# Linear attention and a gated feed-forward layer on one core: block 0's decay in its mask, WO by column halves, projection 0 in half tiles

## The chip, the cores and the metric

The kernel runs on one core of a Trainium2 chip. Its engines each run their own instruction stream in order: TensorE (PE; its weight loads are listed as PEld), VectorE (DVE), ScalarE (ACT), GpSimd (POOL) and SyncE (SP). SP, ACT and POOL can issue DMA transfers; they share 16 DMA engines. Engines wait for each other through semaphores. The metric is the time of one execution on the device in microseconds (us); lower is better.

## The reference

```python
for b in range(nb):                      # attention, block after block
    qb, kb, vb = (q[:, :, sl], k[:, :, sl], v[:, :, sl])
    intra = einsum('bhic,bhjc->bhij', qb, kb) * Dmask      # lam ** (i - j), i >= j
    intra = einsum('bhij,bhjd->bhid', intra, vb)
    inter = einsum('bhid,bhde->bhie', qb * lam_pow, kv_state)
    out[:, :, sl] = intra + inter
    kv_state = lam_block * kv_state + einsum('bhsd,bhse->bhde', kb * rev_pow, vb)
x = out.transpose(0, 2, 1, 3).reshape(B * S, H * D)        # 3072 x 512
gate = 1.0 / (1.0 + np.exp(-(x @ w_gate)))
val = x @ w_val
result = gate * val @ w_out                                # 3072 x 512
```

Batch 4, 8 heads, sequence 768, head size 64; `w_gate` and `w_val` are 512 x 1536, `w_out` is 1536 x 512. `lam` holds one decay per head, from 0.97 to 0.99. All tensors are float32 in memory; the kernel computes its matmuls in bf16.

## The kernel before

The sequence is cut into six blocks of C = 128 positions (`NSTEP`). A block takes all four batches at once, so that its feed-forward work has 512 tokens. For each block n the stages are:

- Load q, k, v as bf16 (`load`, L83, on POOL's queue). Block 0's k of batches 0 and 1 come as float32 on SP (`load_hw`, L134) and are cast on VectorE (`cast_hw`, L226).
- Transpose q and k: by TensorE for blocks 0 and 1 (`t_`, L202, evacuated by `e_q` and `e_k`), by DMA from block 2 on (`xbar`, L229, issued on SP). `e_q` (L209) scales q by lam^(i+1) (`lamq`).
- Scores (`piece_s`, L238) into two PSUM banks per batch; product with the mask on VectorE (`piece_m`, L249). Because q carries lam^(i+1), the mask needs only lam^(-j-1) below the diagonal (`make_mask`, L190, from `pk` and `tri`).
- Attention output: the part from the state (`piece_i`, L255, not for block 0) and the part from v (`piece_a`, L266); evacuation to XT (`piece_x`, L278); the new state (`piece_c`, L285, with k scaled by `kds` in `piece_kd`, L116, on ScalarE).
- Gate and value (`piece_gv`, L308): twelve units, each four gate matmuls and four value matmuls of 512 columns, a sigmoid on ScalarE and a product on VectorE. The PSUM pool `ps_ff` has three banks, which gate, value and output tiles take in turn; attention has a pool of five (`ps_at`).
- Projection (`piece_po`, L324): for each batch tile 12 matmuls against WO, a copy on ScalarE, an output DMA on SP.

The order on each engine is the program order, written out by hand. First comes the prologue (L340 to L379): block 0's attention for batches 0 and 1, then 2 and 3, with filler matmuls (`zeros`) between. Then the remaining loads are put on POOL's queue (L383 to L395). Then comes `plan` (L412 to L502), a list of units with small pieces behind each: block 0's gate and value units, with block 1's transposes, scores and masks behind units 7 to 11 and its attention (`att(1)`) behind unit 11; four of block 1's units; projection 0; block 1's other units; then block by block. In blocks 2 to 5 the attention of the next block stands behind unit 11 and before the projection.

POOL's queue in order: q, k, q, v of block 0; WG and WV in five parts; block 1's k and q with WG/WV parts between; v of block 1; WO in two halves by rows of 128 (`load_wo`, L107); k and q of block 2. A DMA on this queue was issued, from the ninth on, only after the one eight before it had landed: for instance, the issue at 42.45 us waited for block 1's v. From block 2 on, `next_loads` (L403) puts two DMA transposes on SP, then two small copies on POOL (`gate`, L399) that wait for them, and behind these the loads of the next v, k and q. SP also issues the outputs, so transposes and outputs stand in one queue.

`tables_late` (L182) computes `kds` and `dec`, loads the sigmoid table and swaps the two 64-partition halves of `lamq` and `dec` by four DMAs on SP into `lamqs` and `decs`, which batches 2 and 3 use from block 1 on (`swapped`).

Of the kernel before, what the change touches and what calls it, by code (L numbers as in the profile page):

```python
# [16 lines left out]
def kernel(  # L17
# [26 lines left out]
    hwp = ctx.enter_context(tc.tile_pool(name="hwp", bufs=4))  # L44
# [26 lines left out]
    def swapped(n, b):  # L71
        return n > 0 and b >= NB2
# [7 lines left out]
    def rows_of(u):  # L80
        return slice(u * 64, (u + 1) * 64)
# [22 lines left out]
        nc.gpsimd.dma_start(out=WG[:, :, fs], in_=wg_r[:, :, fs])  # L104
        nc.gpsimd.dma_start(out=WV[:, :, fs], in_=wv_r[:, :, fs])

    def load_wo(f0, f1):  # L107
        fs = slice(f0, f1)
        nc.gpsimd.dma_start(out=WO[:, fs, :], in_=wo_r[:, fs, :])

    KD = {}

# [13 lines left out]
    jn = const.tile([128, 2], FP32, tag="jn")  # L126
    ip1 = const.tile([128, C], FP32, tag="ip1")
    tri = const.tile([128, C], FP32, tag="tri")
    Sb = stp.tile([128, HP, B, 64], BF16, tag="Sb", name="Sb")
    lam_bc = const.tile([128, H], FP32, tag="lam_bc")  # L130

# [2 lines left out]
    def load_hw(c, b, eng):  # L134
# [9 lines left out]
    nc.scalar.preload_act_table_set("natural_log_exp_and_others")  # L144
    nc.vector.memset(ident, 0.0)
    nc.vector.memset(Sb, 0.0)  # L146
    nc.vector.memset(tri, 0.0)
# [14 lines left out]
    load_gv(2, 4)  # L162
    load_gv(4, 6)

    lnp = const.tile([128, HP], FP32, tag="lnp")
# [3 lines left out]
    lamq = const.tile([128, HP, C], BF16, tag="lamq")  # L169
    for hp in range(HP):  # L170
        nc.scalar.activation(lamq[:, hp, :], ip1, AF.Exp, scale=lnp[:, hp:hp + 1])
    lamqs = const.tile([128, HP, C], BF16, tag="lamqs")
    lnl = const.tile([128, H], FP32, tag="lnl")
    nc.scalar.activation(lnl, lam_bc, AF.Ln)
    pk = const.tile([128, H], FP32, tag="pk")
    nc.scalar.activation(pk, lnl, AF.Exp, scale=jn[:, 0:1])
    kds = const.tile([128, H], FP32, tag="kds")
    dec = const.tile([128, HP], FP32, tag="dec")
    decs = const.tile([128, HP], FP32, tag="decs")
# [10 lines left out]
    def make_mask():  # L190
        nc.vector.tensor_tensor(
            out=mask, in0=tri.unsqueeze(1).unsqueeze(1).to_broadcast([128, 2, HP, C]),
            in1=pk.rearrange("p (hp u) -> p u hp", u=2).unsqueeze(3).to_broadcast([128, 2, HP, C]),
            op=ALU.mult)

# [6 lines left out]
    def t_(c, n, bs):  # L202
        ps = ps_at.tile([128, len(bs), HP, C], BF16, name="t" + c, tag="ps")
        for i, b in enumerate(bs):
            for hp in range(HP):
                nc.tensor.transpose(ps[:, i, hp, :], T_[c, n][:, b, 2 * hp:2 * hp + 2, :], ident)  # L206
        (tqs if c == "q" else tks)[n, bs[0]] = ps

    def e_q(n, bs):  # L209
        w = len(bs)  # L210
        src = tqs[n, bs[0]] if n < FIRST_XBAR else QT[n][:, bs[0]:bs[0] + w]
        t = trsb.tile([128, 2, HP, C], BF16, tag="QS", name="QS")
        nc.vector.tensor_tensor(out=t[:, :w], in0=src,  # L213
                                in1=(lamqs if swapped(n, bs[0]) else lamq).unsqueeze(1).to_broadcast([128, w, HP, C]), op=ALU.mult)
        for i in range(w):
            QS[n, bs[i]] = t[:, i]

# [8 lines left out]
    def cast_hw(c, b):  # L226
        nc.vector.tensor_copy(T_[c, 0][:, b], H32[c, b])
# [21 lines left out]
    def piece_m(n, b):  # L249
        MT[n, b] = mtp.tile([128, 2, HP, C], BF16, tag="MT", name="MT")  # L250
        for u in range(2):
            nc.vector.tensor_tensor(out=MT[n, b][:, u], in0=SP[n, b][u],  # L252
                                    in1=mask[:, 1 - u if swapped(n, b) else u], op=ALU.mult)

    def piece_i(n):  # L255
        for b in range(B):
# [67 lines left out]
    def piece_po(n, tt, cuts=(0, 512)):  # L324
        ob = osb.tile([128, DM], FP32, tag="ob", name="ob")
        rows = out[tt * S + n * C:tt * S + (n + 1) * C, :]
        for j, (c0, c1) in enumerate(zip(cuts, cuts[1:])):
            po = ps_ff.tile([128, DM], FP32, name="po", tag="ff")
            for ft in range(NFT):
                nc.tensor.matmul(po[:, :c1 - c0], lhsT=HT[n, ft][:, tt * 128:(tt + 1) * 128],  # L330
                                 rhs=WO[:, ft, c0:c1], start=(ft == 0), stop=(ft == NFT - 1))
            if j:
                nc.vector.tensor_copy(ob[:, c0:c1], po[:, :c1 - c0])
            else:
                nc.scalar.copy(ob[:, c0:c1], po[:, :c1 - c0])  # L335
            nc.sync.dma_start(out=rows[:, c0:c1], in_=ob[:, c0:c1])

# [6 lines left out]
            nc.tensor.matmul(zps, lhsT=Sb[:, 0, 0:2, :], rhs=Sb[:, 0:2], start=True, stop=True)  # L344

    zeros(9)
    for b in range(2):
        cast_hw("k", b)
        t_("k", 0, [b])
        e_k(0, [b])  # L350
        zeros(3 if b == 0 else 0)
    make_mask()
    for b in range(2):
        t_("q", 0, [b])
        e_q(0, [b])
    zeros(1)
    for b in range(2):
        piece_s(0, [b])
        piece_m(0, b)
    t_("k", 0, [2, 3])  # L360
    e_k(0, [2, 3], parts=2)
    zeros(2)
    t_("q", 0, [2, 3])
    e_q(0, [2, 3])
    tables_late()
    zeros(3)
    for b in range(2, 4):
        piece_s(0, [b])
        piece_m(0, b)
    for b in range(2):  # L370
        piece_a(0, [b])
        piece_x(0, [b], nc.scalar)
# [44 lines left out]
    def gv(n, ft, *more):  # L417
        unit(lambda: piece_gv(n, ft), *more)

    def po(n, tt, *more, cuts=(0, 512)):  # L420
        unit(lambda: piece_po(n, tt, cuts), *more)

    def pair(f, n, bp):
        return lambda: f(n, [2 * bp, 2 * bp + 1])
# [38 lines left out]
    for n in range(1, NSTEP):  # L463
        nx = n + 1
        more = {i: [] for i in range(NFT)}
# [10 lines left out]
        if nx < NSTEP - 1:  # L476
            more[5].append(lambda nx=nx: make_kd(nx))
        if n == 1:
            for ft in range(4):
                gv(1, ft, *[lambda: next_loads(2)] if ft == 3 else [])  # L480
            for tt in range(B):
                po(0, tt, *[lambda: next_loads(3)] if tt == 3 else [])
            gv(1, 4, *more[3])
            gv(1, 5)
            gv(1, 6, *more[4])
            gv(1, 7, *more[5])
            gv(1, 8, *more[6])
            gv(1, 9, *more[7])
            gv(1, 10, *more[8])
            gv(1, 11, *more[9], *more[10], *more[11])  # L490
        else:
            for ft in range(NFT):
                gv(n, ft, *more[ft])
        for tt in range(B):
            last = n == NSTEP - 1 and tt == B - 1
            more = [lambda n=n: next_loads(n + 3)] if tt == B - 1 and n + 3 < NSTEP else []
            po(n, tt, *more, cuts=(0, 256, 512) if last else (0, 512))

    for f, more in plan:
        f()  # L500
# [32 lines left out]
```

## Time and profile before

| What | Value |
|---|---|
| Median of 3 runs | 230.18 us (230.18 to 230.3) |
| Profiled execution, time | 230.23 us |
| Profiled execution, span from first to last instruction | 228.4 us |
| Mean granted TensorE clock | 1.000 |
| First gate matmul (L313) of block 0 | 17.82 us |
| First gate matmul of block 1 | 45.81 us |
| Projection 0 (L330) | 52.73 us, 10.5 us long |
| Last copy of the output (L333) | 225.36 us, 0.42 us long |
| DMA packets under 512 B | 94,080 of 104,083 |
| Bytes on POOL's queue (q0) and on SP's (q1) | 13.90 MB and 11.15 MB |

The page divides the span into engines' busy time, and then gives groups of instructions by line: how many, their busy time, the mean of one, and the idle time before them with what ended it. The costliest groups on the engines beside TensorE:

```profile
L322 DVE TENSOR_TENSOR ht<-sg,vp 128x512 bf16<-128x512 bf16 x72 | 49.4, 687 | 105.0 <-PE vp L319 101.4
L316 ACT ACTIVATE sg<-gp 128x512 bf16<-128x512 f32 x72 | 42.9, 596 | 66.0 <-PE gp L313 63.3
L335 ACT COPY ob<-po 128x512 f32<-128x512 f32 (+1 forms) x24 | 13.8, 576 | 47.3 <-PE po L330 47.3
L252 DVE TENSOR_TENSOR MT<-sp,mask 128x512 bf16<-128x512 f32 x48 | 30.4, 682 | 0.6 <-PE sp L244 0.5
```

The number before the bar is the count; then come busy us and the mean in ns; then the idle us and their releaser. Such idle time costs nothing where the engine isn't the one that sets the end.

### The profile page before, as it was taken

How to read it: one execution, taken by the hardware profiler on the slowest of the kernel's cores; microseconds unless marked ns; L12 is line 12 of the kernel's file. 1: busy time of each engine (PE TensorE's matmuls, PEld its weight loads, DVE VectorE, ACT ScalarE, POOL GpSimd, SP SyncE). 2: the span in 40 equal slices, each digit the busy share in tenths (PEclk: the TensorE clock that was granted, in tenths of full speed). 3: DMA queues.
4: the chain of work that ended last, by engine and by line, in shares of the span. 5: the costliest groups of instructions: out<-in, count | busy, mean ns of one | idle time of the engine just before them, and what ended most of it. 6: DMA issues, size and time to landing. Idle time of an engine off the chain costs nothing.

```text
span 228.4 us, 4108 instructions
## 1 busy us (share of the span) xinstructions
PE 218.3 (96%) x1642; PEld 107.2 (47%) x1668; DVE 100.9 (44%) x177; ACT 98.2 (43%) x207; POOL 57.9 (25%) x73
## 2 busy tenths in 40 slices
PE   7779999999999999999999999999999999999994
PEld 2444455544444644444554444454444454444443
DVE  2863367862038730368530368630268600343300
ACT  5465635932245832338542438642433342433221
POOL 7958669200192039004900030000000000000000
PEclk9999999999999999999999999999999999999999
DMA  7999999999999969994993739003100012100022
GB/s 113 156 166 196 174 173 176 201 181 160 221 158 152 192 99 146 211 167 78 137 160 122 168 65 91 3 27 114 46 0 3 0 37 103 46 0 0 3 92 93
DMA packets 104083, 25.31 MB, mean 111 GB/s; under 512 B 94080, under 2 KB 101120, under 8 KB 104064
## 3 DMA queue, kind: packets, MB, share of 16 engines
q0 software_dynamic: 81280, 13.90, 82.0%
q1 hardware_dynamic: 22640, 11.15, 20.7%
q8 instruction: 13, 0.21, 0.4%
q14 instruction: 6, 0.05, 0.1%
q10 hardware_dynamic: 144, 0.00, 0.0%
HBM read 28.32 MB, written 6.29 MB: 151 GB/s over the span
## 4 chain that ended last, share of the span: by engine, by line
PE 89%; DVE 3%; DMA 3%; issue 2%; POOL 1%; POOLq 0%; DVEq 0%
PE po L330 27%; PE vp L319 27%; PE gp L313 27%; DMA qb<-in_q_dram 3%; PE sp L244 3%; PE op L273 2%; DVE MT L252 2%; PE op L262 1%; PE cp L291 1%; DVE XT L283 1%; PE tq L206 1%; POOL kb L92 0%; PE tk L206 0%; DVE QS L213 0%; POOL qb L92 0%
## 5 line engine op out<-in xcount | busy, mean ns | idle before, releaser
L322 DVE TENSOR_TENSOR ht<-sg,vp 128x512 bf16<-128x512 bf16 x72 | 49.4, 687 | 105.0 <-PE vp L319 101.4
L319 PE MATMUL vp<-XT,WV 128*128 128x512 bf16 x284 | 73.5, 379 | 0.4
L313 PE MATMUL gp<-XT,WG 128*128 128x512 bf16 x274 | 72.1, 379 | 1.4 <-DVE XT L283 0.5
L316 ACT ACTIVATE sg<-gp 128x512 bf16<-128x512 f32 x72 | 42.9, 596 | 66.0 <-PE gp L313 63.3
L330 PE MATMUL po<-WO,ht 128*128 128x512 bf16 (+1 forms) x294 | 62.7, 370 | 0.4 <-issue 0.2
L330 PEld LDWEIGHTS <-ht 128*128 128x128 bf16 x300 | 29.0, 98 | 32.3
L319 PEld LDWEIGHTS <-WV 128*128 128x128 bf16 x288 | 28.2, 98 | 34.0
L313 PEld LDWEIGHTS <-WG 128*128 128x128 bf16 x288 | 27.0, 98 | 32.6 <-issue 0.8
L335 ACT COPY ob<-po 128x512 f32<-128x512 f32 (+1 forms) x24 | 13.8, 576 | 47.3 <-PE po L330 47.3
L252 DVE TENSOR_TENSOR MT<-sp,mask 128x512 bf16<-128x512 f32 x48 | 30.4, 682 | 0.6 <-PE sp L244 0.5
L121 ACT ACTIVATE kd<-kb,kds 128x128 bf16<-128x128 bf16 (+1 forms) x72 | 23.7, 402 | 0.0
L401 POOL COPY gates<-kt 128x1 bf16<-128x1 bf16 x4 | 0.7, 187 | 55.8 <-DMA kt<-kb 55.8
L283 ACT CAST XT<-op 128x512 bf16<-128x512 f32 x21 | 11.0, 596 | 5.5 <-PE op L273 5.5
L92 POOL DMA_DIRECT2D vb<-in_v_dram x7 | 10.7, 1530 | 2.6 <-issue 1.2
L98 POOL DMA_DIRECT2D qb<-in_q_dram x10 | 9.0, 916 | 3.1 <-DMA vb<-in_v_dram 2.1
L344 PE MATMUL zps<-Sb 128*128 128x512 bf16 x22 | 8.1, 499 | 1.6 <-DVE Sb L146 1.5
L98 POOL DMA_DIRECT2D kb<-in_k_dram x10 | 8.9, 902 | 1.0 <-DMA WG<-in_moe_w_gate_dram 0.6
L92 POOL DMA_DIRECT2D qb<-in_q_dram x7 | 8.4, 1202 | 0.8 <-POOLq L517 0.8
L273 PE MATMUL op<-MT,vb 128*64 128x128 bf16 x192 | 7.1, 221 | 0.4 <-DVE MT L252 0.3
L92 POOL DMA_DIRECT2D kb<-in_k_dram x6 | 7.0, 1166 | 0.0
L300 DVE SCALAR_TENSOR_TENSOR Sb<-Sb,dec,cp 128x128 bf16<-128x128 bf16 x16 | 5.5, 342 | 3.2 <-PE cp L291 3.2
L273 PEld LDWEIGHTS <-vb 128*64 128x64 bf16 x192 | 5.7, 110 | 1.6 <-DMA vb<-in_v_dram 0.7
(47 smaller groups left out, 83.2 us busy)
## 6 DMA issues: line engine op xcount, KB each, us to landing
out_dram<-ob SPq DMA_DIRECT2D x23, 256.0 KB, 2.0
vb<-in_v_dram POOLq DMA_DIRECT2D x5, 512.0 KB, 7.6
qb<-in_q_dram POOLq DMA_DIRECT2D x7, 256.0 KB, 9.4
kb<-in_k_dram POOLq DMA_DIRECT2D x6, 256.0 KB, 8.6
WO<-in_moe_w_out_dram POOLq DMA_DIRECT2D x2, 768.0 KB, 13.7
WG<-in_moe_w_gate_dram POOLq DMA_DIRECT2D x5, 256.0 KB, 8.6
WV<-in_moe_w_val_dram POOLq DMA_DIRECT2D x5, 256.0 KB, 9.1
kb<-in_k_dram POOLq DMA_DIRECT2D x10, 128.0 KB, 9.7
```

Of the source, the lines that this page charges most:

```text
L92: nc.gpsimd.dma_start(out=T_[c, n][:, b0:nat], in_=src[b0:nat, :, sl, :].rearrange("b h s d -> s (b h) d"))
L98: nc.gpsimd.dma_start(out=T_[c, n][:, m:b1, u::2, :], in_=src[m:b1, 1 - u::2, sl, :].rearrange("b h s d -> s (b h) d"))
L121: nc.scalar.mul(KD[n][:, at, i, :], T_["k", n][:, at, i, :], kds[:, h:h + 1])
L252: nc.vector.tensor_tensor(out=MT[n, b][:, u], in0=SP[n, b][u], in1=mask[:, 1 - u if swapped(n, b) else u], op=ALU.mult)
L273: nc.tensor.matmul(OP[n, b][rows_of(w), hp, :], lhsT=T_["v", n][:, b, h, :], rhs=MT[n, b][:, slot(n, b, h) % 2, hp, :], start=(n == 0 and ...
L283: (e.tensor_copy if e is nc.vector else e.copy)(XT[n][:, :, b, :], OP[n, b])
L313: nc.tensor.matmul(gp, lhsT=WG[:, mt, fs], rhs=x[:, mt, :], start=(mt == 0), stop=(mt == NMT - 1))
L316: nc.scalar.activation(sg, gp, AF.Sigmoid)
L319: nc.tensor.matmul(vp, lhsT=WV[:, mt, fs], rhs=x[:, mt, :], start=(mt == 0), stop=(mt == NMT - 1))
L322: nc.vector.tensor_mul(HT[n, ft], sg, vp)
L330: nc.tensor.matmul(po[:, :c1 - c0], lhsT=HT[n, ft][:, tt * 128:(tt + 1) * 128], rhs=WO[:, ft, c0:c1], start=(ft == 0), stop=(ft == NFT - 1))
L335: nc.scalar.copy(ob[:, c0:c1], po[:, :c1 - c0])
```

## The change

Six things change.

1. Block 0's mask holds the whole decay, lam^(i-j) on and below the diagonal. `exponents` writes (i - j) * ln(lam), or about -30000 above the diagonal, with four small VectorE instructions for each half of the heads; `powers` takes the exponential on ScalarE. Block 0's q is then only copied, not scaled, one batch at a time, by VectorE or ScalarE. POOL gets one more iota (`dij`) and one more select (`neg`) ahead of block 0's second k load, VectorE one more memset.
2. The order of the prologue changes: `pk` moves to `tables_late`, which comes earlier; the sigmoid table is loaded after batch 2's q; the half swap becomes `swap_halves`, four DMAs issued by ScalarE behind block 0's first gate unit; the mask of the later blocks is made in two halves behind units 1 and 3.
3. The last batch's attention output of block 0 goes into two PSUM banks, and ScalarE and VectorE copy one each to XT.
4. WO is loaded by column halves. On POOL's queue all gate and value parts but the last move ahead of block 1's q and k; then WO's first half, batches 2 and 3 of k and q, WO's second half, and v.
5. Projection 0 is computed as eight half tiles (all four batches by the first 256 columns, then by the second), directly after block 0's gate and value units. The rest of block 1's transposes, scores, masks, scaled k and its attention stand between these half tiles.
6. Block 1's gate and value units follow as one run of twelve, and the pieces of block 2 that stood behind units 3 to 9 stand one unit later than in other blocks. `next_loads(2)` stands behind unit 2 and `next_loads(3)` behind unit 8.

The pool `hwp` has two buffers instead of four. The core of the diff:

```diff
-    def load_wo(f0, f1):
-        fs = slice(f0, f1)
-        nc.gpsimd.dma_start(out=WO[:, fs, :], in_=wo_r[:, fs, :])
+    def load_wo(c0, c1):
+        nc.gpsimd.dma_start(out=WO[:, :, c0:c1], in_=wo_r[:, :, c0:c1])
...
+    nc.gpsimd.iota(dij, pattern=[[1, C]], base=0, channel_multiplier=-1,
+                   allow_small_or_imprecise_dtypes=True)
+    nc.gpsimd.affine_select(out=neg, in_=neg, compare_op=ALU.is_ge, fill=-30000.0, base=0,
+                            pattern=[[1, C]], channel_multiplier=-1)
     nc.gpsimd.iota(ip1, pattern=[[1, C]], base=1, channel_multiplier=0,
                    allow_small_or_imprecise_dtypes=True)
     load(0, "k", 2, 4)
...
+    def exponents(u):
+        for hp in range(HP):
+            h = 2 * hp + u
+            nc.vector.scalar_tensor_tensor(out=mask0[:, u, hp], in0=dij, scalar=lnl[:, h:h + 1],
+                                           in1=neg, op0=ALU.mult, op1=ALU.add)
+
+    def powers(u):
+        nc.scalar.activation(mask0[:, u], mask0[:, u], AF.Exp)
+
     def tables_late():
+        nc.scalar.activation(pk, lnl, AF.Exp, scale=jn[:, 0:1])
         nc.scalar.activation(kds, lnl, AF.Exp, scale=jn[:, 1:2])
         nc.scalar.activation(dec, lnp, AF.Exp, scale=float(C))
-        nc.scalar.preload_act_table_set("sigmoid_and_others")
-        for o, i in ((lamqs, lamq), (decs, dec)):
-            for u in range(2):
-                nc.sync.dma_start(out=o[rows_of(u)], in_=i[rows_of(1 - u)])
+
+    def swap_halves():
+        for u in range(2):
+            o, i = rows_of(u), rows_of(1 - u)
+            nc.scalar.dma_start(out=lamq2[o, 1], in_=lamq2[i, 0])
+            nc.scalar.dma_start(out=dec2[o, 1], in_=dec2[i, 0])
...
-    def e_q(n, bs):
+    def e_q(n, bs, eng=None):
...
+        if n == 0:
+            (nc.scalar.copy if eng is nc.scalar else nc.vector.tensor_copy)(t[:, :w], src)
+        else:
...
     t_("k", 0, [2, 3])
     e_k(0, [2, 3], parts=2)
     zeros(2)
-    t_("q", 0, [2, 3])
-    e_q(0, [2, 3])
-    tables_late()
-    zeros(3)
+    t_("q", 0, [2])
+    e_q(0, [2], nc.scalar)
+    t_("q", 0, [3])
+    e_q(0, [3], nc.vector)
+    nc.scalar.preload_act_table_set("sigmoid_and_others")
+    zeros(1)
...
-    piece_a(0, [3])
-    piece_x(0, [3], nc.vector)
-    zeros(2)
+    ops = [ps_at.tile([128, HP // 2, C], FP32, name="op", tag="ps") for _ in range(2)]
+    for g in range(2):
+        for hp in range(2 * g, 2 * g + 2):
+            for w in range(2):
+                nc.tensor.matmul(ops[g][rows_of(w), hp % 2, :], lhsT=T_["v", 0][:, 3, 2 * hp + w, :],
+                                 rhs=MT[0, 3][:, w, hp, :], start=(hp % 2 == 0), stop=(hp % 2 == 1),
+                                 skip_group_check=True)
+    nc.scalar.copy(XT[0][:, 0:2, 3, :], ops[0])
+    nc.vector.tensor_copy(XT[0][:, 2:4, 3, :], ops[1])
...
     load_gv(6, 8)
+    load_gv(8, 10)
     load(1, "k", 0, 2)
     load(1, "q", 0, 2)
-    load_gv(8, 10)
+    load_gv(10, 12)
+    load_wo(0, 256)
     load(1, "k", 2, 4)
     load(1, "q", 2, 4)
-    load_gv(10, 12)
+    load_wo(256, 512)
     load(1, "v")
-    load_wo(0, 6)
-    load_wo(6, 12)
     load(2, "kq")
...
+    behind[0].append(swap_halves)
+    behind[1].append(lambda: make_mask(0))
+    behind[3].append(lambda: make_mask(1))
     behind[5] = [pair(piece_c, 0, 0), pair(piece_c, 0, 1)]
-    behind[7] = [trans(1, 0)]
-    behind[8] = [pair(piece_s, 1, 0), m_(1, 0), m_(1, 1)]
-    behind[9] = [trans(1, 1), kd(1, 0)]
-    behind[10] = [pair(piece_s, 1, 1), m_(1, 2), m_(1, 3), kd(1, 2), kd(1, 4)]
-    behind[11] = [kd(1, 6), att(1)]
+    behind[8] = [trans(1, 0)]
+    behind[9] = [pair(piece_s, 1, 0), m_(1, 0)]
+    behind[10] = [m_(1, 1)]
     for ft in range(NFT):
         gv(0, ft, *behind[ft])
+    after = {(0, 1): [kd(1, 0)], (0, 2): [trans(1, 1)], (0, 3): [pair(piece_s, 1, 1), m_(1, 2), kd(1, 2)],
+             (1, 0): [m_(1, 3), kd(1, 4)], (1, 1): [kd(1, 6)], (1, 2): [att(1)]}
+    for j in range(2):
+        for tt in range(B):
+            po(0, tt, *after.get((j, tt), []), c=(256 * j, 256 * (j + 1)))
...
         if n == 1:
-            for ft in range(4):
-                gv(1, ft, *[lambda: next_loads(2)] if ft == 3 else [])
-            for tt in range(B):
-                po(0, tt, *[lambda: next_loads(3)] if tt == 3 else [])
...
+            more[4:11] = more[3:10]
+            more[3] = []
+            more[2].append(lambda: next_loads(2))
+            more[8].append(lambda: next_loads(3))
```

The new prologue up to batch 3's scores, in its order:

```python
zeros(9); exponents(0); powers(0); cast_hw("k", 0); t_("k", 0, [0]); e_k(0, [0])
exponents(1); cast_hw("k", 1); zeros(3); powers(1)
t_("q", 0, [0]); e_q(0, [0], nc.vector); t_("q", 0, [1]); e_q(0, [1], nc.scalar)
t_("k", 0, [1]); e_k(0, [1]); tables_late()
piece_s(0, [0]); piece_m(0, 0); piece_s(0, [1]); piece_m(0, 1)
```

More of the change, by code (lines that the diff above doesn't have):

```diff
@@ L43 @@
     qkv = ctx.enter_context(tc.tile_pool(name="qkv", bufs=5))
-    hwp = ctx.enter_context(tc.tile_pool(name="hwp", bufs=4))
+    hwp = ctx.enter_context(tc.tile_pool(name="hwp", bufs=2))
     qtp = ctx.enter_context(tc.tile_pool(name="qtp", bufs=3))
@@ L128 @@
     tri = const.tile([128, C], FP32, tag="tri")
+    dij = const.tile([128, C], FP32, tag="dij")
+    neg = const.tile([128, C], FP32, tag="neg")
     Sb = stp.tile([128, HP, B, 64], BF16, tag="Sb", name="Sb")
@@ L146 @@
     nc.vector.memset(Sb, 0.0)
+    nc.vector.memset(neg, 0.0)
     nc.vector.memset(tri, 0.0)
     make_identity(nc, ident, nomemset=True)
+    nc.gpsimd.iota(dij, pattern=[[1, C]], base=0, channel_multiplier=-1,
+                   allow_small_or_imprecise_dtypes=True)
+    nc.gpsimd.affine_select(out=neg, in_=neg, compare_op=ALU.is_ge, fill=-30000.0, base=0,
+                            pattern=[[1, C]], channel_multiplier=-1)
     nc.gpsimd.iota(ip1, pattern=[[1, C]], base=1, channel_multiplier=0,
@@ L163 @@
     load_gv(4, 6)
+    lnl = const.tile([128, H], FP32, tag="lnl")
+    nc.scalar.activation(lnl, lam_bc, AF.Ln)
     lnp = const.tile([128, HP], FP32, tag="lnp")
@@ L168 @@
         nc.scalar.activation(lnp[us, :], lam_bc[us, u::2], AF.Ln)
-    lamq = const.tile([128, HP, C], BF16, tag="lamq")
+    lamq2 = const.tile([128, 2, HP, C], BF16, tag="lamq2")
+    lamq, lamqs = lamq2[:, 0], lamq2[:, 1]
     for hp in range(HP):
         nc.scalar.activation(lamq[:, hp, :], ip1, AF.Exp, scale=lnp[:, hp:hp + 1])
-    lamqs = const.tile([128, HP, C], BF16, tag="lamqs")
-    lnl = const.tile([128, H], FP32, tag="lnl")
-    nc.scalar.activation(lnl, lam_bc, AF.Ln)
     pk = const.tile([128, H], FP32, tag="pk")
-    nc.scalar.activation(pk, lnl, AF.Exp, scale=jn[:, 0:1])
@@ L177 @@
     kds = const.tile([128, H], FP32, tag="kds")
-    dec = const.tile([128, HP], FP32, tag="dec")
-    decs = const.tile([128, HP], FP32, tag="decs")
+    dec2 = const.tile([128, 2, HP], FP32, tag="dec2")
+    dec, decs = dec2[:, 0], dec2[:, 1]
+    mask0 = const.tile([128, 2, HP, C], FP32, tag="mask0")
     mask = const.tile([128, 2, HP, C], FP32, tag="mask")
+    def exponents(u):
[3 more added lines that the diff above has]
+                                           in1=neg, op0=ALU.mult, op1=ALU.add)
@@ L190, in make_mask @@
-    def make_mask():
+    def swap_halves():
[3 more added lines that the diff above has]
+            nc.scalar.dma_start(out=dec2[o, 1], in_=dec2[i, 0])
+    def make_mask(u):
         nc.vector.tensor_tensor(
-            out=mask, in0=tri.unsqueeze(1).unsqueeze(1).to_broadcast([128, 2, HP, C]),
-            in1=pk.rearrange("p (hp u) -> p u hp", u=2).unsqueeze(3).to_broadcast([128, 2, HP, C]),
-            op=ALU.mult)
+            out=mask[:, u], in0=tri.unsqueeze(1).to_broadcast([128, HP, C]),
+            in1=pk[:, u::2].unsqueeze(2).to_broadcast([128, HP, C]), op=ALU.mult)
@@ L212, in e_q @@
         t = trsb.tile([128, 2, HP, C], BF16, tag="QS", name="QS")
-        nc.vector.tensor_tensor(out=t[:, :w], in0=src,
-                                in1=(lamqs if swapped(n, bs[0]) else lamq).unsqueeze(1).to_broadcast([128, w, HP, C]), op=ALU.mult)
+        if n == 0:
+            (nc.scalar.copy if eng is nc.scalar else nc.vector.tensor_copy)(t[:, :w], src)
+        else:
+            nc.vector.tensor_tensor(
+                out=t[:, :w], in0=src,
+                in1=(lamqs if swapped(n, bs[0]) else lamq).unsqueeze(1).to_broadcast([128, w, HP, C]),
+                op=ALU.mult)
         for i in range(w):
@@ L252, in piece_m @@
             nc.vector.tensor_tensor(out=MT[n, b][:, u], in0=SP[n, b][u],
-                                    in1=mask[:, 1 - u if swapped(n, b) else u], op=ALU.mult)
+                                    in1=(mask if n else mask0)[:, 1 - u if swapped(n, b) else u],
+                                    op=ALU.mult)
     def piece_i(n):
@@ L322, in piece_gv, with piece_po @@
         nc.vector.tensor_mul(HT[n, ft], sg, vp)
[L324 to L336, printed above, removed]
+    OB = {}
+    def piece_po(n, tt, c0, c1, eng):
+        if (n, tt) not in OB:
+            OB[n, tt] = osb.tile([128, DM], FP32, tag="ob", name="ob")
+        po = ps_ff.tile([128, DM], FP32, name="po", tag="ff")
+        for ft in range(NFT):
+            nc.tensor.matmul(po[:, :c1 - c0], lhsT=HT[n, ft][:, tt * 128:(tt + 1) * 128],
+                             rhs=WO[:, ft, c0:c1], start=(ft == 0), stop=(ft == NFT - 1))
+        o = OB[n, tt][:, c0:c1]
+        (eng.copy if eng is nc.scalar else eng.tensor_copy)(o, po[:, :c1 - c0])
+        nc.sync.dma_start(out=out[tt * S + n * C:tt * S + (n + 1) * C, c0:c1], in_=o)
     zps = ps_ff.tile([128, DM], FP32, name="zps", tag="ff")
@@ L346 @@
     zeros(9)
[L347 to L359, printed above, removed]
+    exponents(0)
+    powers(0)
+    cast_hw("k", 0)
+    t_("k", 0, [0])
+    e_k(0, [0])
+    exponents(1)
+    cast_hw("k", 1)
+    zeros(3)
+    powers(1)
+    t_("q", 0, [0])
+    e_q(0, [0], nc.vector)
+    t_("q", 0, [1])
+    e_q(0, [1], nc.scalar)
+    t_("k", 0, [1])
+    e_k(0, [1])
+    tables_late()
+    piece_s(0, [0])
+    piece_m(0, 0)
+    piece_s(0, [1])
+    piece_m(0, 1)
     t_("k", 0, [2, 3])
@@ L369 @@
         piece_m(0, b)
+    zeros(2)
     for b in range(2):
@@ L418, in gv, with po @@
         unit(lambda: piece_gv(n, ft), *more)
-    def po(n, tt, *more, cuts=(0, 512)):
-        unit(lambda: piece_po(n, tt, cuts), *more)
+    def po(n, tt, *more, c=(0, DM), eng=nc.scalar):
+        unit(lambda: piece_po(n, tt, *c, eng), *more)
     def pair(f, n, bp):
@@ L453 @@
         behind[ft] = [kd(0, 2 * ft)]
+    behind[0].append(swap_halves)
+    behind[1].append(lambda: make_mask(0))
+    behind[3].append(lambda: make_mask(1))
     behind[5] = [pair(piece_c, 0, 0), pair(piece_c, 0, 1)]
-    behind[7] = [trans(1, 0)]
-    behind[8] = [pair(piece_s, 1, 0), m_(1, 0), m_(1, 1)]
-    behind[9] = [trans(1, 1), kd(1, 0)]
-    behind[10] = [pair(piece_s, 1, 1), m_(1, 2), m_(1, 3), kd(1, 2), kd(1, 4)]
-    behind[11] = [kd(1, 6), att(1)]
+    behind[8] = [trans(1, 0)]
+    behind[9] = [pair(piece_s, 1, 0), m_(1, 0)]
+    behind[10] = [m_(1, 1)]
     for ft in range(NFT):
         gv(0, ft, *behind[ft])
+    after = {(0, 1): [kd(1, 0)], (0, 2): [trans(1, 1)], (0, 3): [pair(piece_s, 1, 1), m_(1, 2), kd(1, 2)],
[3 more added lines that the diff above has]
+            po(0, tt, *after.get((j, tt), []), c=(256 * j, 256 * (j + 1)))
     for n in range(1, NSTEP):
         nx = n + 1
-        more = {i: [] for i in range(NFT)}
+        more = [[] for i in range(NFT)]
         if nx < NSTEP:
@@ L475 @@
                 more[6 + i].append(kd(nx, 2 * i))
-        if nx < NSTEP - 1:
             more[5].append(lambda nx=nx: make_kd(nx))
         if n == 1:
-            for ft in range(4):
-                gv(1, ft, *[lambda: next_loads(2)] if ft == 3 else [])
-            for tt in range(B):
-                po(0, tt, *[lambda: next_loads(3)] if tt == 3 else [])
[L483 to L493, printed above, removed]
-        for tt in range(B):
-            last = n == NSTEP - 1 and tt == B - 1
-            more = [lambda n=n: next_loads(n + 3)] if tt == B - 1 and n + 3 < NSTEP else []
-            po(n, tt, *more, cuts=(0, 256, 512) if last else (0, 512))
+            more[4:11] = more[3:10]
+            more[3] = []
+            more[2].append(lambda: next_loads(2))
+            more[8].append(lambda: next_loads(3))
+        for ft in range(NFT):
+            gv(n, ft, *more[ft])
+        for tt in range(B):
+            if n == NSTEP - 1 and tt == B - 1:
+                po(n, tt, c=(0, 256))
+                po(n, tt, c=(256, 512), eng=nc.vector)
+            else:
+                more = [lambda n=n: next_loads(n + 3)] if tt == B - 1 and n + 3 < NSTEP else []
+                po(n, tt, *more)
     for f, more in plan:
```

## The prediction

> **What bounds the kernel now.** I read the engine shares first, then the chain of waits in order of time, then the timeline of single engines around the two places where the chain leaves TensorE. The page's first rows:
>
> ```profile
> PE 218.3 (96%) x1642; PEld 107.2 (47%) x1668; DVE 100.9 (44%) x177; ACT 98.2 (43%) x207; POOL 57.9 (25%) x73
> PEclk9999999999999999999999999999999999999999
> ```
>
> TensorE is busy 96% at full clock, so only what TensorE waits for can be won. The chain (start, length, what):
>
> ```profile
> 4.64 7.40 DMA qb<-in_q_dram
> 12.09 0.64 PE tq L206 x8
> 12.75 0.70 DVE QS L213
> 13.49 0.43 PE sp L244 x8
> 13.92 2.48 DVE MT L252 x4
> 16.53 0.43 PE op L273 x8
> 16.98 0.70 DVE XT L283
> 17.82 1.02 PE gp L313 x4
> ...
> 41.32 1.89 DVE MT L252 x3
> 43.25 0.60 PE op L262 x29
> 43.85 0.59 PE op L273 x16
> 44.46 0.48 DVE XT L283
> 45.07 0.69 DVE XT L283
> ```
>
> See two stretches. Until 17.82 the chain is the prologue: q of batches 2 and 3 lands at 12.09, then 5.73 us pass until the first gate matmul. From 42.43 (last L319 matmul of block 0) to 45.81 (first L313 of block 1) it is block 1's attention, 3.34 to 3.38 us. Block 2 does the same work in 2.32 (77.36 to 80.63 against 41.51 to 45.81, both from the start of the last L319 group, less the group's own 0.96). After 46 the chain is TensorE nearly without gaps. The loads are the second thing to see:
>
> ```profile
> 42.45 0.88 POOL L98 DMA_DIRECT2D qb<-in_q_dram  x1 [2.14 <-DMA vb<-in_v_dram]
> ...
> 53.74 3.19 SPq L232 DMA_TRANSPOSE kt<-kb  x1
> 57.12 3.14 SPq L232 DMA_TRANSPOSE qt<-qb  x1
> ...
> 62.17 0.19 POOL L401 COPY gates<-qt 128x1 bf16<-128x1 bf16 x1 [1.87 <-DMA qt<-qb]
> ```
>
> Block 1's v lands at 42.4, block 2's k at 53.7, its q at 57.1, and its transposed q at 62.17. The windows of 2 us give 155 to 159 GB/s while q, k, v load, 195 to 197 while WG/WV load, 207 while WO loads, from 3 to 58 us without a break: the load queue has no spare room there.
>
> **Prologue.** Removed from the chain: the 128x1024 scaling on VectorE (L213, 0.69 us, behind eight transposes, 0.64). Added: two plain copies of half the size, one on each engine. Only the first four transposes stand before the first copy (0.39 us for four, the L206 rows at 7.46). The ScalarE copy takes 0.59 (L222, 128x512), the VectorE one 0.42 (L213, 128x512) and runs beside it. The scores of batch 2 can start at landing + 0.39 + 0.06 + 0.59 + 0.06 = 1.10, against 1.40 now: 0.3 saved. Four mask products follow (2.62 to the next matmul, unchanged). The last XT (0.69 + 0.15, starting 0.45 after its first matmul) becomes two 128x256 copies (0.37 ScalarE, 0.42 VectorE, the output rows of that size): first matmul to gate matmul falls from 1.29 to about 1.0. But batch 3's product also sits behind batch 2's, which waits for v (15.86), then needs 0.25 of issue and one filler of 0.22: not before 16.33 against 16.53 now. So 0.2 + 0.3 = **0.5 saved**, first gate matmul at 17.3.
>
> What is added lies beside this. VectorE gets eight 128x128 scalar-tensor products; the nearest row is L300, 0.26 each back to back, 1.1 us for four: the first cast moves from 5.07 to about 5.4, the second to about 8.4, and the transpose of it stands behind q, which lands at 8.17. ScalarE gets two 128x512 Exps (0.6 each; L316 has that size), from 5.8 and 7.5, in idle time. The first two batches' products should end on VectorE at 12.15 (now 11.99), still before its copy at 12.75. The table load (1.28) moves behind the copy, to 13.1 to 14.4, before XT at 14.58. On the POOL queue an iota and a select (0.19 and 0.25 between starts) push every later issue by 0.45 us. If landings followed, the 0.5 would be gone. But landings are 1.8 to 2.1 us apart and issues 1.2 to 1.6: the transfers queue, so the delay should vanish. Against it the two 64 KB lamqs transfers (issued 5.70) leave this stretch: 0.13 MB at 155 GB/s, up to 0.8 us earlier. Bounds of the prologue: 0 to 1.1 saved.
>
> **swap_halves on ScalarE.** Four DMA issues, now on SP (0.54 to 0.59 and 0.46 to 0.60 each), go behind the first kd. The rows there:
>
> ```profile
> 18.88 0.60 ACT L316 ACTIVATE sg<-gp 128x512 bf16<-128x512 f32 x1 [1.98 <-PE gp L313]
> 19.38 0.90 ACT L121 ACTIVATE kd<-kb,kds 128x256 bf16<-128x256 bf16 x2
> 20.61 0.60 ACT L316 ACTIVATE sg<-gp 128x512 bf16<-128x512 f32 x1 [0.34 <-PE gp L313]
> ```
>
> ScalarE is idle only 0.34 us before the second sigmoid. Behind the issues wait that sigmoid, and behind it the third value product, which takes the gate's PSUM bank (three banks): it wants to start at 22.30. At 0.5 each the sigmoid starts at 20.28 + 2.0 and ends at 22.88: TensorE waits 0.55. At 0.33 (the SP output issues) nothing; at 0.6, 0.95. The Trainium skill, "DMA: Bandwidth & Descriptors", Issuing engines are not separate DMA queues, says that another issuing engine saves only issue time, "usually small relative to the DMA itself". That speaks against the move: no bandwidth comes, and the issue time falls on the engine that frees TensorE's banks. Taken as small the sum would be 0.55 better; I take the row: **0.55 lost**. The next sigmoids catch up, since kd plus sigmoid is 1.4 of each 1.73 us. The two half masks (half of L191's 1.21) fit VectorE's idle 1.04.
>
> **Block 1 in projection 0.** The last two mask pairs and the kd products (2.43 + 1.27 on ScalarE) no longer stand between gate work and attention: each gets a half tile of 12 x 256 columns, 1.31 us (the last projection's two copies, 224.05 and 225.36). Attention falls to block 2's 2.3, and XT and the state updates hide under the last half tile. **1.1 saved** (bounds 0.9 to 1.3). TensorE work is only moved: 96 half matmuls at 0.109 against 48 at 0.216, 0.1 lost. ScalarE pays eight copies of 0.37 for four of 0.58, 0.6 in all; a kd unit is 1.27 + 0.37 against 1.31 of TensorE, covered by the three banks. What is late next is data.
>
> **Loads.** WO is now wanted at the projection's start. Before it: last gate work at 42.44 - 0.9 (transposes) - 0.65 (scores) - 0.5 + 0.55 = 40.9. Landing: v's 42.4 less 6.8 us for k, q and v of 1.05 MB at 155, plus half of WO, 0.79 MB at 197 = 4.0, gives 39.6. On the column halves (512-byte rows) the same page's Specifications call 512 B enough for line rate; the rows say 197 GB/s at that size (WG) against 207 for WO's 1 KB, 0.4 us over both halves; I use the rows. Second half: 39.6 + 3.4 (k, q) + 4.0 = 47.0, wanted at 40.9 + 4 x 1.31 + 0.9 + 0.65 = 47.7. But the outputs of projection 0 now go out beside these loads. Their price: from v's issue to the next k's landing takes 11.8 us in block 2 (62.59 to 74.40) and 13.9 in block 3 (83.82 to 97.68), where four output tiles run beside it: 2.05 us for four tiles, 0.26 per half. So 47.8: no slack. Block 1's v: 47.0 + 3.4 + 1.3 = 51.7, wanted at 52.2. Transposed q: 62.17 + 2.05 = 64.2, wanted at 64.9 (scores at 65.6 less 0.69). SP also holds the transposes behind eight outputs, the last at about 55.5; k lands near there anyway. I count 0, bounds 0 to 1.0.
>
> **Sum.** -0.5 + 0.55 - 1.1 + 0.1 = -0.95 on 228.4 us. The profiled execution took 230.23, so 229.28; the median of the runs is 0.05 lower than that execution, within what I round: **229.3**. The last block and its output are untouched.
>
> **Rivals.** (a) *No wait behind the issues* (they cost 0.33, or run under the last kd) and q lands up to 0.4 earlier without lamqs: 0.95 + 0.55 + 0.4 = 1.9 saved, **228.3**. For: the first 12 us are full of transfers; against: the same transfers' own rows. (b) *A load is hidden no longer*: WO's second half, or the queue shifted by POOL's 0.45, costs 0.6 more: **229.9**. For: slack of -0.1 to 0.7 at three places. Against: later stretches reach 387 GB/s with outputs. (c) *Outputs displace loads byte for byte* at 4.4 us per MB (the first loads of k, 0.52 MB, held the queue back some 2.3 us): 4.6 + 0.4 us, transposed q at 67.2, scores at 67.9 against 66.7 now less the moved unit (68.43 - 1.73): slower by 1.2, **231.4**. It decides from a landing of transposed q later than 66.0. Against it: block 3's measured 2.05. (d) *It doesn't do what it says*: the prologue gains 0 because POOL's delay reaches v; part of (b).
>
> **How the numbers follow.** Forecast 0.5 (own range 228.8 to 229.8), (a) 0.22, (b) with (d) 0.2, (c) 0.08. A difference under 0.2% (0.46 us) can't be told from none. Faster: nearly all of the forecast and (a), two fifths of (b): 0.8. Same: the rest of (b) and the forecast's edge, 0.12. Slower 0.08. The range of 228.3 to 230.4 leaves out (c) and the far end of (a).
>
> **What would show it.** Right: first L313 matmul near 17.3; a TensorE gap near 22.5 before the third L319 group, with the second sigmoid late behind four ScalarE issues; projection 0 from about 41 to 51 without a wait for MT or XT; attention of block 1 in 2.3. Wrong: no gap at 22.5 (a); waits on WO, vb or qt between 41 and 66 (b, c); first L313 at 17.8 with v as its releaser (d).

## The result and the profile after

| | before | after |
|---|---|---|
| Median | 230.19 us (4 runs) | 229.37 us (229.13 to 229.38, 4 runs) |
| Ratio | | 0.9961, 95% interval 0.9944 to 0.9978 |
| Profiled execution: time, span | 230.23, 228.4 us | 229.37, 227.6 us |
| First gate matmul | 17.82 us | 16.08 us |
| Last projection begins (TensorE) | 214.77 us | 213.66 us |
| Last output copy begins | 225.36 us | 224.25 us |

The change makes the kernel 0.8 us faster (the interval allows 0.5 to 1.3). The forecast was 229.3 us. The engine shares hardly move; the chain that ended last does. From the page of the changed kernel, the first row, and the chain by engine and by line:

```profile
PE 216.2 (95%) x1689; PEld 110.9 (49%) x1713; DVE 101.6 (45%) x186; ACT 100.9 (44%) x216; POOL 59.5 (26%) x75
...
PE 77%; DMA 15%; POOL 5%; issue 2%; DVE 0%; POOLq 0%
PE po L354 25%; PE vp L342 23%; PE gp L336 22%; DMA WO<-in_moe_w_out_dram 7%; DMA qb<-in_q_dram 5%; DMA WG<-in_moe_w_gate_dram 3%; PE op L296 2%; PE sp L266 2%; PE op L285 1%; POOL vb L92 1%; POOL kb L92 1%; PE cp L314 1%; POOL WG L104 1%; POOL qb L92 1%; POOL WV L105 1%
```

Before, 3% of the chain was DMA; now it is 15%, and half of that is WO. The chain in order of time shows what this means (start, length, what):

```profile
20.51 11.52 DMA qb<-in_q_dram
32.03 0.62 issue
32.65 14.94 DMA WO<-in_moe_w_out_dram
47.59 0.04 issue
47.63 4.09 PE po L354 x36
51.73 0.57 PE op L285 x32
52.30 1.01 PE op L296 x32
53.31 0.50 PE cp L314 x32
```

Up to 47.63 us the end is no longer set by TensorE but by the load queue. What TensorE had won before that point ends in a wait. TensorE's timeline around the wait (start, length, what, in brackets the idle time before and its releaser):

```profile
39.30 4.11 PE L354 MATMUL po<-WO,ht 128*128 128x256 bf16 x36
43.24 0.61 PE L223 MATMUL tk<-ident,kb 128*128 128x128 bf16 x8
43.69 0.61 PE L223 MATMUL tq<-ident,qb 128*128 128x128 bf16 x8
44.13 1.47 PE L354 MATMUL po<-WO,ht 128*128 128x256 bf16 x12
45.54 0.62 PE L266 MATMUL sp<-QS,KS 64*128 64x128 bf16 x16
47.63 4.09 PE L354 MATMUL po<-WO,ht 128*128 128x256 bf16 x36 [1.48 <-DMA WO<-in_moe_w_out_dram]
51.66 0.64 PE L285 MATMUL op<-QS,Sb 64*64 64x128 bf16 x32
52.23 1.08 PE L296 MATMUL op<-MT,vb 128*64 128x128 bf16 x32
53.14 0.67 PE L314 MATMUL cp<-vb,kd 128*64 128x64 bf16 x32
53.75 1.48 PE L354 MATMUL po<-WO,ht 128*128 128x256 bf16 x12
```

The first half of WO is just in time at 39.30. The second comes 1.48 us late. Block 1's attention itself now takes 2.09 us (51.66 to 53.75), as was hoped, against 3.34 before, from the first to the second of these lines of the old kernel:

```profile
42.47 0.40 PE L262 MATMUL op<-QS,Sb 64*64 64x128 bf16 x3
...
45.81 1.04 PE L313 MATMUL gp<-XT,WG 128*128 128x512 bf16 x3 [0.18 <-DVE XT L283]
```

At the beginning of the last projection TensorE is 1.11 us ahead of the old kernel, but the span is only 0.8 shorter. The other 0.3 us lies behind the last copy: 2.6 us from its end (225.78) to the span's end before, 2.9 after. Nothing in the change touches that stretch; in the runs below it varies from 2.6 to 2.9.

### The profile page after: what moved, and what is told of

Read it like the earlier page. It is cut to its first block, busy times and chain, and to the rows that moved or that the text cites. A ratio compares the mean times of both kernels' runs of the same rounds, so it can differ in the third digit from the quotient of the medians.

```text
span 227.6 us, 4227 instructions
## 1 busy us (share of the span) xinstructions
PE 216.2 (95%) x1689; PEld 110.9 (49%) x1713; DVE 101.6 (45%) x186; ACT 100.9 (44%) x216; POOL 59.5 (26%) x75
## 4 chain that ended last, share of the span: by engine, by line
PE 77%; DMA 15%; POOL 5%; issue 2%; DVE 0%; POOLq 0%
PE po L354 25%; PE vp L342 23%; PE gp L336 22%; DMA WO<-in_moe_w_out_dram 7%; DMA qb<-in_q_dram 5%; DMA WG<-in_moe_w_gate_dram 3%; PE op L296 2%; PE sp L266 2%; PE op L285 1%; POOL vb L92 1%; POOL kb L92 1%; PE cp L314 1%; POOL WG L104 1%; POOL qb L92 1%; POOL WV L105 1%
## 5 line engine op out<-in xcount | busy, mean ns | idle before, releaser
L354 PE MATMUL po<-WO,ht 128*128 128x512 bf16 (+1 forms) x343 | 63.6, 342 | 1.8 <-DMA WO<-in_moe_w_out_dram 1.5
L354 PEld LDWEIGHTS <-ht 128*128 128x128 bf16 x348 | 33.5, 98 | 29.8 <-issue 1.5
L357 ACT COPY ob<-po 128x512 f32<-128x512 f32 (+1 forms) x28 | 14.4, 515 | 45.3 <-PE po L354 45.3
L323 DVE SCALAR_TENSOR_TENSOR Sb<-Sb,dec,cp 128x128 bf16<-128x128 bf16 x32 | 8.6, 342 | 3.3 <-PE cp L314 3.3
L366 PE MATMUL zps<-Sb 128*128 128x512 bf16 x19 | 6.5, 469 | 1.6 <-DVE Sb L147 1.5
L296 PE MATMUL op<-MT,vb 128*64 128x128 bf16 x184 | 6.5, 221 | 0.0
```

The lines of the kernel that those rows point to most:

```text
L296: nc.tensor.matmul(OP[n, b][rows_of(w), hp, :], lhsT=T_["v", n][:, b, h, :], rhs=MT[n, b][:, slot(n, b, h) % 2, hp, :], start=(n == 0 and ...
L357: (eng.copy if eng is nc.scalar else eng.tensor_copy)(o, po[:, :c1 - c0])
```

## The experiments

My theory after this was: from 40 us on the load queue sets the pace. So the prologue's gain would be hidden in the changed kernel, and what counts is when the transfers land and how much stands in the queue before them. The rival was that the parts simply add, with the wait for WO as a fixed price of the new order. Each run below was compared with runs of the old kernel on the same chip (medians of 230.27 and 230.30 there). The edits are shown against the changed kernel, and the longer ones in part.

### The prologue alone

All of the change's items 1 to 3, with the old loads, the old WO rows, the old projection and the old order of units:

```diff
     load_gv(6, 8)
-    load_gv(8, 10)
     load(1, "k", 0, 2)
     load(1, "q", 0, 2)
-    load_gv(10, 12)
-    load_wo(0, 256)
+    load_gv(8, 10)
...
-    behind[8] = [trans(1, 0)]
+    behind[7] = [trans(1, 0)]
...
```

> The new prologue (block 0's mask, the two-engine copies, the late half swap on ScalarE) with the old loads and the old order of units. Theory A (in the changed kernel the second half of WO sets the pace, so the prologue's gain is hidden there): the first gate matmul stays near 16.1 us, nothing waits for WO, and most of the 1.74 us arrives at the end: 228.5 to 228.9 us, faster than the full change. Theory B (the gain is given back in any order, because block 1's v lands at 42.4 us and the old kernel wants it at 43.9): wait for v of about 1 us, 229.2 to 229.6 us.

229.09 us (228.96 to 229.56), ratio 0.9954 (0.9941 to 0.9966). Neither range was met. The first gate matmul came at 15.99, and nothing waited for WO or for v. But a third load was late. TensorE's timeline of this run:

```profile
37.05 1.04 PE L337 MATMUL gp<-XT,WG 128*128 128x512 bf16 x4 [0.30 <-DMA WG<-in_moe_w_gate_dram]
38.41 1.04 PE L343 MATMUL vp<-XT,WV 128*128 128x512 bf16 x4 [0.33 <-DMA WV<-in_moe_w_val_dram]
...
44.65 1.04 PE L337 MATMUL gp<-XT,WG 128*128 128x512 bf16 x3 [0.44 <-DVE XT L307]
```

The last part of the gate and value weights stands behind block 1's k and q in the old queue. TensorE reaches it at 36.6 (0.9 of transposes after 35.69), starts at 37.05 and loses as much again before the value group; and block 1 starts at 44.65 instead of 45.81. So 1.83 won at the first gate matmul are 1.16 there, and 1.2 at the end. Even so the prologue alone gives as much as the whole change, as far as these runs can tell: the two intervals overlap.

### The loads and the order of units alone

The old prologue and the old half swap on SP, with the change's items 4 to 6:

```diff
-    behind[0].append(swap_halves)
-    behind[1].append(lambda: make_mask(0))
-    behind[3].append(lambda: make_mask(1))
...
-    exponents(0)
-    powers(0)
...
```

> The old prologue and the old early half swap on SP, with the new loads, half tiles and order of units. Theory A (loads set the pace): first gate matmul at 17.8 us, second half of WO lands near 47.6 us as in the full change, TensorE reaches it at 47.7 to 47.9 us, so the wait is under 0.3 us and the time is 229.2 to 229.6 us, the same as the full change. Theory B (parts add; the wait of 1.5 us is a fixed cost of this plan): 230.9 to 231.2 us.

230.03 us (229.59 to 230.42, 13 runs), ratio 0.999 (0.9982 to 0.9998). The first gate matmul is at 17.88. TensorE's timeline:

```profile
47.66 4.10 PE L330 MATMUL po<-WO,ht 128*128 128x256 bf16 x36
...
66.05 0.62 PE L243 MATMUL sp<-QS,kt 64*128 64x128 bf16 x16 [0.37 <-DVE QS L212]
```

The second half of the projection starts at 47.66 with no wait, against 47.63 in the full change. 1.8 us of prologue made no difference at this point: that part of theory A is shown, and theory B (231 us) falls. The forecast of the time missed by 0.6, since a second load comes next: block 2's scores wait for its scaled q, and VectorE waited 0.46 us for the transposed q. VectorE's line of this run, then that of the full change, where the q was scaled without a wait:

```profile
65.21 0.69 DVE L212 TENSOR_TENSOR QS<-qt,lamq 128x1024 bf16<-128x1024 bf16 x1 [0.46 <-DMA qt<-qb]
```

```profile
64.58 0.69 DVE L233 TENSOR_TENSOR QS<-qt,lamq 128x1024 bf16<-128x1024 bf16 x1
```

So the prologue is not worth nothing in the new order. It is worth 0.66 us (230.03 to 229.37), a good third of what it wins at the first gate matmul, and the traces say how it gets past WO: the queue itself runs earlier. The issue of a load that waits for WO's first half comes at 40.05 here and at 39.54 in the full change. Which part of the old prologue holds the queue back was not separated; the early half swap alone does not (39.59 in the next run, and the q scaled at 64.73).

The parts do not add: 1.2 alone and 0.27 alone (hardly more than nothing, by its interval) are 0.8 together.

### The half swap as early as before

```diff
-            nc.scalar.dma_start(out=lamq2[o, 1], in_=lamq2[i, 0])
+            nc.sync.dma_start(out=lamq2[o, 1], in_=lamq2[i, 0])
...
     tables_late()
+    swap_halves()
     piece_s(0, [0])
...
-    behind[0].append(swap_halves)
```

> The full change, but the four half-swap transfers are issued by SP as early as in the old kernel. Theory A (those 0.13 MB held back the first loads): q of batches 2 and 3 lands near 12.0 us instead of 11.2, v near 15.8 instead of 14.6, first gate matmul at 17.0 to 17.3 us; WO's wait shrinks to 0.3 to 0.6 us and the time stays 229.2 to 229.5 us. Theory B (the earlier landings come from the later POOL issues or from elsewhere): q at 11.2 us, first gate at 16.1 us, time unchanged as well.

229.61 us (229.34 to 229.88), ratio 0.9969 (0.9957 to 0.998), not told apart from the full change. TensorE's timeline:

```profile
11.92 0.62 PE L225 MATMUL tq<-ident,qb 128*128 128x128 bf16 x8 [1.26 <-DMA qb<-in_q_dram]
...
15.40 0.41 PE L298 MATMUL op<-MT,vb 128*64 128x128 bf16 x8
...
47.32 4.09 PE L356 MATMUL po<-WO,ht 128*128 128x256 bf16 x36 [0.58 <-DMA WO<-in_moe_w_out_dram]
```

In the full change the first of these lines has 11.16, the second 14.65, and the first gate matmul is at 16.08; here it is at 16.83. So 0.13 MB of half swap in the first 12 us held up block 0's q and v by about 0.75 us each. And the 0.75 us do not reach the end: the wait for WO shrinks from 1.48 to 0.58. Theory A holds on both counts.

### Projection 0's outputs held back

Each output tile is sent whole, after its second half, so no output runs before WO has landed:

```diff
-        nc.sync.dma_start(out=out[tt * S + n * C:tt * S + (n + 1) * C, c0:c1], in_=o)
+        w0 = 0 if n == 0 else c0
+        if n > 0 or c1 == DM:
+            nc.sync.dma_start(out=out[tt * S + n * C:tt * S + (n + 1) * C, w0:c1], in_=OB[n, tt][:, w0:c1])
```

> The full change, but projection 0 sends each output tile whole, after its second half, so that no output runs before WO's second half has landed. Theory A (outputs displace loads, 0.26 us per half tile): WO lands 0.8 to 1.0 us earlier, near 46.7 us, the wait falls from 1.48 to 0.5 to 0.7 us; then block 2's transposed q (64.5 us) is late by 0.3 to 0.7, so the time is 228.9 to 229.3 us. Theory B (outputs run in spare room): WO lands at 47.6 us and nothing changes, 229.4 us.

228.54 us (228.24 to 228.63), ratio 0.9923 (0.9909 to 0.9936). TensorE's timeline:

```profile
46.36 4.09 PE L354 MATMUL po<-WO,ht 128*128 128x256 bf16 x36 [0.49 <-DMA WO<-in_moe_w_out_dram]
...
64.87 0.62 PE L266 MATMUL sp<-QS,kt 64*128 64x128 bf16 x16 [0.56 <-DVE QS L233]
```

WO's second half landed 1.27 us earlier: the outputs of four half tiles had delayed it by that. Three of them were issued 3.6 us or more before the landing in the full change, the fourth 1.5 us before, so each cost 0.3 to 0.4 us. The next wait is the one seen in the second run, block 2's transposed q, 0.56 us here. The waits fit theory A; the time is better than its range by 0.4 us.

### Block 2's pieces one unit later

```diff
-            more[4:11] = more[3:10]
-            more[3] = []
+            more[5:11], more[11] = more[3:9], more[9] + more[11]
+            more[3], more[4] = [], []
```

on top of the held outputs.

> As the run with the whole output tiles (228.54 us), and block 2's scaling of q, scores and masks stand one more unit later behind block 1's units. Theory A (after WO, block 2's transposed q is what TensorE waits for, 0.56 us): that wait goes, nothing new appears, 227.9 to 228.2 us. Theory B (another transfer or VectorE's queue holds TensorE at the same point, for instance block 2's attention at the end of block 1's units, whose masks now come later): 228.4 to 228.7 us.

228.21 us (228.03 to 228.23), ratio 0.9911 (0.9896 to 0.9926), at the edge of theory A's range. The wait for the scaled q is gone, and between the projection and block 2's scores TensorE stands still for WO alone:

```profile
46.51 4.09 PE L354 MATMUL po<-WO,ht 128*128 128x256 bf16 x36 [0.48 <-DMA WO<-in_moe_w_out_dram]
```

The last projection begins 0.47 us earlier than in the run before (212.54 against 213.01).

### WO's second half as two transfers

```diff
-    load_wo(256, 512)
+    load_wo(256, 512, 0, NFT // 2)
+    load_wo(256, 512, NFT // 2, NFT)
```

on top of the last two, with `load_wo` taking a range of row blocks.

> As the run before it, and WO's second half is loaded as two transfers of six row blocks each. Theory A (TensorE needs only the first rows when the second half of the projection starts): the wait of 0.49 us goes, 227.4 to 227.8 us. Theory B (what follows is bound by the data all the same: block 1's v or transposed q is late by what WO gave back): 227.9 to 228.2 us.

227.37 us (227.33 to 227.91), ratio 0.988 (0.9866 to 0.9893): 1.2% faster than the old kernel, and 0.9% faster than the changed one measured in the same set (229.38, below). The chain by engine of this run and TensorE's timeline around the projection:

```profile
PE 92%; DMA 3%; issue 2%; POOL 1%; ACT 1%; DVE 0%; POOLq 0%
```

```profile
45.30 0.62 PE L266 MATMUL sp<-QS,KS 64*128 64x128 bf16 x16
45.85 4.10 PE L354 MATMUL po<-WO,ht 128*128 128x256 bf16 x36
49.88 0.64 PE L285 MATMUL op<-QS,Sb 64*64 64x128 bf16 x32
```

From 15.98 us on TensorE waits nowhere as much as 0.1 us for a load, and DMA's share of the chain is back at 3%. Only now do the prologue's gain (1.84 us here) and that of block 1's attention (1.24) both reach the end nearly whole: the last projection begins at 211.89, 2.88 us before the old kernel's.

### The address of the float32 tiles

The two casts of k took 0.41 us in the changed kernel, 0.98 and 0.87 in the old one. `hwp` with four buffers again, all else as changed:

```diff
-    hwp = ctx.enter_context(tc.tile_pool(name="hwp", bufs=2))
+    hwp = ctx.enter_context(tc.tile_pool(name="hwp", bufs=4))
```

> The full change with four buffers in the pool of the float32 k tiles instead of two, which moves the addresses of what is allocated after them and nothing else. Theory A (the casts of these tiles, 0.41 us against 0.92 before, are fast because of where things lie): casts of 0.9 us, first gate matmul still near 16.1 us because they are off the chain, 229.3 to 229.5 us. Theory B (they are fast because of when they run or what runs beside them): casts stay at 0.41, same time.

229.38 us, ratio 0.9962 (0.9949 to 0.9974), and casts of 0.41 and 0.42. So it isn't the number of buffers, nor the addresses that this number shifts; theory A falls as far as these go. This run is also the changed kernel measured once more, with a wait for WO of 1.57 us.

## Why the prediction was right

The total was right, but three of its terms were wrong and made up for each other, so that it came out this close is luck. Counted on TensorE's timeline, up to the last projection:

| Step | Predicted | Measured | From |
|---|---|---|---|
| Prologue | -0.5 | -1.74 | first gate matmul, 17.82 to 16.08 |
| Issues on ScalarE | +0.55 | +0.05 | third value group, 20.44 instead of 20.39 |
| Wait for WO's second half | 0 | +1.48 | the wait before 47.63 |
| Block 1's attention | -1.1 | -1.25 | 3.34 to 2.09 |
| Half tiles | +0.1 | +0.1 | 8 x 1.31 against 48 x 0.216 |
| Sum | -0.95 | -1.36 | |

The timeline's own difference at the last projection is -1.11; the 0.25 between is in gaps of 0.05 to 0.16 us that I did not follow one by one. Behind the last copy, 0.3 us come back, to -0.8. Of the signs named beforehand, those of two rivals came together: no gap before the third value group (a), and a wait on WO (b).

**Why the errors cancelled.** The prediction worked out when WO's second half lands (47.8, measured 47.6) and when TensorE wants it (47.7, in fact about 46.1), and called it "no slack". The second of these is where it failed: the wait is 1.48, outside its bounds of 0 to 1.0. As long as TensorE comes before the load, the second half of the projection starts when the load lands. The prologue's extra 1.24 us and the 0.5 us not lost on ScalarE only made TensorE wait longer. The second and third runs show it: with TensorE free at 47.66 or held 0.58 us there, the projection's second half starts at 47.66 and 47.32. The landing was the term that decided. WO's first half came as worked out (39.6; the issue that waits for it is at 39.54). The second came out right by two more errors that cancel: without outputs the sum gave 47.0, and in the fourth run TensorE got it at 46.36; for the outputs the sum added 0.8, and they cost 1.27. Their price, read from a stretch where outputs ran beside the same loads, was of the right size but low: 0.26 us for a half tile, against 0.3 to 0.4.

**Prologue.** The 1.74 us are 0.93 from an earlier landing of q (11.16 against 12.09), 0.33 from the copies and 0.52 from the last XT, less 0.04. Three parts were undersized. The late half swap was left at "up to 0.8 us earlier" and counted at nothing; the third run puts it at about 0.75. The later POOL issues delayed nothing, as argued: q landed 0.2 us earlier than before even with the swap in its old place (11.92 against 12.09). The copies saved 0.33 (1.07 from landing to scores against 1.40; 0.3 predicted). The last XT saved 0.52 instead of 0.29 (0.77 from the product's first matmul to the gate matmul against 1.29): the first gate matmul was released by ScalarE's copy alone, since it reads only the first bank's half; VectorE's copy ended at 16.19. TensorE's lines of the changed kernel:

```profile
15.31 0.41 PE L413 MATMUL op<-MT,vb 128*64 128x128 bf16 x8 [0.25 <-DVE MT L274]
16.08 1.02 PE L336 MATMUL gp<-XT,WG 128*128 128x512 bf16 x4 [0.35 <-ACT XT L416]
```

The 0.2 us that v was to take away were not lost, since v came earlier as well.

**The issues on ScalarE.** The step that failed is the start of the issues. The sum lets the first begin when kd ends (the 20.28 in "20.28 + 2.0"), so that all four come on top. ScalarE's timeline in the changed kernel:

```profile
17.14 0.60 ACT L339 ACTIVATE sg<-gp 128x512 bf16<-128x512 f32 x1 [1.11 <-PE gp L336]
17.28 0.52 ACTq L205 DMA_DIRECT2D lamq<-lamq  x1
17.64 0.50 ACT L120 ACTIVATE kd<-kb,kds 128x256 bf16<-128x256 bf16 x1
17.85 0.60 ACTq L206 DMA_DIRECT2D dec<-dec  x1
18.03 0.50 ACT L120 ACTIVATE kd<-kb,kds 128x256 bf16<-128x256 bf16 x1
18.48 0.62 ACTq L205 DMA_DIRECT2D lamq<-lamq  x1
19.12 0.62 ACTq L206 DMA_DIRECT2D dec<-dec  x1
19.79 0.60 ACT L339 ACTIVATE sg<-gp 128x512 bf16<-128x512 f32 x1 [1.26 <-PE vp L342]
```

The issues are no cheaper than on SP, 0.52 to 0.62 each. But the first begins while the sigmoid before it still runs, although both kd products stand ahead of it in the program, and the second runs beside these products. Two of four issues lie under work, and the sigmoid ends at 20.39, when the value group wants its bank. This was rival (a)'s mechanism, "run under the last kd". The Trainium skill's "usually small relative to the DMA itself" ("DMA: Bandwidth & Descriptors", Issuing engines are not separate DMA queues) holds here: 0.52 to 0.62 us to issue a 64 KB transfer that lands 5.0 us later. It would have given the better term, though a total of 228.7, further off. But what kept TensorE from waiting is the overlap: the four issues together took 2.4 us.

The same value group shows that the prologue has met the next load. Its weights (WV) landed at 20.24 in the changed kernel, just before the sigmoid's end. In the seventh run, the same kernel at other addresses, the sigmoid ended at 20.22 and the weights came last, 0.30 us after TensorE could have begun. TensorE's weight loads, changed kernel and seventh run:

```profile
20.24 0.72 PEld L342 LDWEIGHTS <-WV 128*128 128x128 bf16 x4 [0.18 <-DMA WV<-in_moe_w_val_dram]
```

```profile
20.52 0.55 PEld L342 LDWEIGHTS <-WV 128*128 128x128 bf16 x4 [0.62 <-DMA WV<-in_moe_w_val_dram]
```

**Rivals.** (b), a load hidden no longer, is what happened, at the place with the least slack; its cost was paid out of gains that I had not counted, which is luck and no part of the argument. (c), outputs that displace loads byte for byte, did not: 0.3 to 0.4 us for 0.13 MB is 2.4 to 3.2 us per MB, against its price of 4.4. The two other close places held as forecast: v was in time, and the transposed q was scaled at 64.58, where 64.9 was the limit; it becomes the next wait as soon as WO comes earlier.

## What to carry to other kernels

When a queue of loads runs without a break, work out for each transfer when it lands and when it is wanted. At the first one that lands late, TensorE waits away what was won ahead of it; only what brings the queue itself forward gets through (0.66 of the prologue's 1.8 us here). There the remedies are in the queue and in the order: send outputs after the late load, split that load so that its first rows can be used, and put work that needs the next load later. These three edits brought 2.0 us on top of the change (229.37 to 227.37), of which 0.8 came from outputs sent later; the change itself had brought 0.8 us.

Two changes that each help alone (1.2 and 0.27 us here) need not add when they use the same slack, so run each alone.

## What the runs showed of the hardware beyond the forecast

- Issuing a DMA on ScalarE overlaps with its arithmetic: the issue at 17.28 began 0.14 us after a 0.60 us sigmoid had begun, and before two activations that stand ahead of it in the program. The row of an issue on ScalarE was not time taken from its arithmetic one for one.
- Two 64 KB and two very small transfers within SBUF delayed block 0's q and v by about 0.75 us; four outputs of 128 KB delayed WO by 1.27 us.
- The cast of a 128x512 float32 tile took 0.41 us in every run where it began after other VectorE work, and 0.87 to 1.01 in the two kernels with the old prologue, where it began as its load landed. The number of buffers has been ruled out, and GpSimd was issuing loads beside the casts in both the old and the changed kernel; the cause is open. The casts are not on the chain.
